# Seven summed block products in place of eight in the second batch's channel up-projection of a fused fp32 kernel

## Chip, cores and metric

The kernel runs on one core of one Trainium2 chip. The metric is the device time of one execution in microseconds (us); lower is better.

## The reference, cut to what matters

Windowed attention over two batches of 768 tokens feeds a gated unit with a spatial mixing matrix, and that feeds a low-rank token mix and a channel network. The change is in the channel network alone:

```python
u = x + (x.T @ U @ V).T                            # (2, 768, 512)
ch = np.maximum(u @ w_ch1, 0.0) @ w_ch2            # w_ch1 512 x 2048, w_ch2 2048 x 512
return u + ch
```

All of it is fp32. The kernel splits each operand into a rounded high part and a low remainder and forms a product from three matrix products: high by high, high by low, low by high.

## The kernel before

The 2048 hidden channels are 16 chunks of 128 (NCH, line 29). The list `seq` (line 821) runs over batch 0's chunks and then batch 1's, 32 steps n in all. In a step, `m4(n, j, bank)` (line 857) makes the hidden activations of one chunk for one half j of the tokens: 4 blocks of 128 input channels by 3 products, 12 matmuls of 384 columns with the weights stationary and `X[b]` moving. ScalarE then writes the rounded ReLU, and VectorE the low part (lines 864 and 865). `m5(n, t)` (line 867) multiplies 128 tokens of the hidden chunk by the chunk's rows of w_ch2: 3 matmuls of 512 columns that accumulate over the 16 chunks in PSUM bank 2+t. After a batch's last chunk VectorE adds y and SyncE stores the result (lines 874 and 875). Banks 0 and 1 take the two halves of m4. The loop of lines 973 to 988 emits m4 of step n and then the six m5 of step n-1.

The weights come from HBM as 64-bit numbers. `ch_decode` (line 839) turns a chunk into fp32, kept in `P["f"]` for both batches; this work ends in batch 0. `ch_split` (line 846) splits a chunk again for each of its two uses: two pieces of 512 columns, in each a rounding on ScalarE and a subtraction on GpSimd, into one of three slots of `P["wch"]`. The first 512 columns of a slot are w_ch1 (`c1`), the other 512 w_ch2 (`c2`).

Order within an engine is the order of emission; engines wait for one another through semaphores alone. The class `Plan` (lines 66 to 189) decides at which point background work such as these splits is put into the engines' streams. It books every instruction on an account of its engine with a price (lines 107 to 120: for VectorE 1.04 ns an element and 70 ns, for GpSimd 2.2 ns an element and 100 ns), with no term for two engines that hinder each other. After each group of three matmuls `tick` (line 162) emits chains, in the order in which they were added, whose engine is booked no more than 400 ns past TensorE's account. `flush` (line 180) emits whatever is left of some chains, one instruction of each in turn.

Of the kernel before, what the change touches and what calls it, by code (L numbers as in the profile page):

```python
# [20 lines left out]
KB = 4  # L21
# [171 lines left out]
def kernel(ctx: ExitStack, tc: tile.TileContext, qk, qt, kn, vab, vn_, gl_,  # L193
# [11 lines left out]
    def body(dense, sb, pp):  # L205
# [5 lines left out]
        def tl(tag, n, name):  # L211
            t = sb.tile([128, n], F32, tag=tag, name=f"{name}_{int(dense)}")
            plan.home[t.tensor.name] = tag
            return t
# [23 lines left out]
        def mm3(o_, l_, r, first, last):  # L238
            mm(o_, l_[0], r[0], first, False)
            mm(o_, l_[0], r[1], False, False)  # L240
            mm(o_, l_[1], r[0], False, last)
            tick()
# [580 lines left out]
        def f_place(c):  # L823

            if c == 0:
                t_ = tl(T_SP, N_SP, "f0")
                P["f"] = [t_[:, 1024 * n:1024 * n + 1024] for n in range(9)]
            elif c == 9:
                t_ = tl("stg", 3072, "f1")
                P["f"] += [t_[:, 1024 * n:1024 * n + 1024] for n in range(3)]  # L830
            elif c == 12:
                P["f"] += [tl(T_WK, N_WK, "f2")[:, 0:1024]]
            elif c == 13:
                t_ = tl(T_UT, N_UT, "f3")
                P["f"] += [t_[:, 1024 * n:1024 * n + 1024] for n in range(3)]
# [3 lines left out]
        def ch_decode(c):  # L839
            f_place(c)  # L840
            f, rw = P["f"][c], P["raw"][c % 2]
            ld = plan.add([o_dma(rw.bitcast(I32), w_ch[c].bitcast(I32))], decoded.get(c - 2, []))
            decoded[c] = [plan.add(decode(rw[:, 1024 * j:1024 * j + 1024], f[:, 512 * j:512 * j + 512]), [ld])
                          for j in range(2)]

        def ch_split(n):
            c = seq[n][1]
            w = [t[:, n % 3] for t in P["wch"]]
            split[n] = [plan.add(splits(w[0][:, 512 * j:512 * j + 512], w[1][:, 512 * j:512 * j + 512],
                                        P["f"][c][:, 512 * j:512 * j + 512], A, G), [decoded[c][j]])  # L850
                        for j in range(2)]

        def chv(n):
            w = [t[:, n % 3] for t in P["wch"]]
# [12 lines left out]
        def m5(n, t):  # L867
            b, c = seq[n]
            _, c2 = chv(n)
            y = P["y"]  # L870
            mm3(bank[2 + t], [P["h1"][n % 2][l][:, 128 * t:128 * t + 128] for l in range(2)], c2,
                n % NCH == 0, n % NCH == NCH - 1)
            if n % NCH == NCH - 1:
                V.tensor_tensor(out=y[b][:, t], in0=bank[2 + t], in1=y[b][:, t], op=ALU.add)
                SP.dma_start(out[b, 128 * t:128 * t + 128, :], y[b][:, t])


        lns, gs = {}, []
# [56 lines left out]
        for t in range(NB):  # L935
# [12 lines left out]
                t3(0, 2 * t - 4, bank[4])  # L948
                t3(0, 2 * t - 3, bank[5])
            tick()  # L950
        P["h1"] = [tl(f"win1{n}", 2048, f"h1{n}") for n in range(2)]
        P["h1"] = [[t[:, l * S:(l + 1) * S] for l in range(2)] for t in P["h1"]]
        flush(split[0])
        m4(0, 0, bank[0])
        t1(1, NB - 1, bank[7])
# [14 lines left out]
        for t in range(3, 6):  # L970
            t3(1, t, bank[5 + t - 3])
        ch_decode(3)
        for n in range(1, 2 * NCH):
            if 1 < n and n + 2 < NCH:
                ch_decode(n + 2)
            if n >= 2:
                flush(split[n])
                m4(n, 0, bank[0])
                tick()
                m4(n, 1, bank[1])  # L980
                tick()
            if n + 1 < 2 * NCH:
                ch_split(n + 1)
            for t in range(NB):
                m5(n - 1, t)
                tick()
        for t in range(NB):
            m5(2 * NCH - 1, t)
        assert not plan.chains

    program(False)
# [56 lines left out]
```

## Time and profile before

| what | us |
|---|---|
| median of 3 runs | 535.81 |
| lowest and highest of them | 533.86 and 538.69 |
| the profiled execution, its own time | 532.87 |
| span of the profiled execution | 531.1 |

The time of an execution holds 1.8 us around the span. PE is TensorE, PEld its weight loads, DVE VectorE, ACT ScalarE, POOL GpSimd, SP SyncE. A row such as "402.31 4.33 PE ... x24" gives the start in us from the span's start, the length of the merged run, and the number of instructions. Nearly all of the kernel's instructions bear line 56, that of a helper, so groups are told apart by the names of their tiles: `bank<-x,wch` is m4, `bank<-wch,h` is m5, `wch` is a weight split, `h` is an eviction of m4.

### The profile page before, as it was taken

How to read it: one execution, taken by the hardware profiler on the slowest of the kernel's cores; microseconds unless marked ns; L12 is line 12 of the kernel's file. 1: busy time of each engine (PE TensorE's matmuls, PEld its weight loads, DVE VectorE, ACT ScalarE, POOL GpSimd, SP SyncE). 2: the span in 40 equal slices, each digit the busy share in tenths (PEclk: the TensorE clock that was granted, in tenths of full speed). 3: DMA queues.
4: the chain of work that ended last, by engine and by line, in shares of the span. 5: the costliest groups of instructions: out<-in, count | busy, mean ns of one | idle time of the engine just before them, and what ended most of it. 6: DMA issues, size and time to landing. Idle time of an engine off the chain costs nothing.

```text
span 531.1 us, 7975 instructions
## 1 busy us (share of the span) xinstructions
PE 504.7 (95%) x2916; PEld 447.5 (84%) x2916; DVE 304.6 (57%) x734; ACT 213.0 (40%) x513; POOL 180.8 (34%) x207
## 2 busy tenths in 40 slices
PE   5768999799999999999999999999999999999994
PEld 4557877689899999888988989899898998989893
DVE  8797789845599743697798867764141101111013
ACT  4878878522454203654444243342212212122120
POOL 5587656610246103220043242423323233231310
PEclk9998999999999999999999999999999999999998
DMA  8657562300421202230126242420030000000003
GB/s 301 220 153 266 167 217 82 121 1 1 122 77 56 61 0 67 112 141 11 69 79 210 107 160 91 148 79 1 0 120 1 0 1 1 1 0 1 0 3 124
DMA packets 13520, 44.74 MB, mean 84 GB/s; under 512 B 1568, under 2 KB 3744, under 8 KB 11424
## 3 DMA queue, kind: packets, MB, share of 16 engines
q1 hardware_dynamic: 13328, 44.14, 24.3%
q8 instruction: 25, 0.41, 0.3%
q14 instruction: 23, 0.19, 0.1%
q10 hardware_dynamic: 144, 0.00, 0.0%
HBM read 40.99 MB, written 3.15 MB: 83 GB/s over the span
## 4 chain that ended last, share of the span: by engine, by line
PE 88%; DVE 8%; ACT 1%; issue 1%; DMA 1%; POOL 0%; ACTq 0%
PE bank L56 88%; DVE prob L56 2%; DVE sm L56 1%; DVE rawin L56 1%; DVE y L56 1%; DVE ptb L56 1%; DMA ni<-in_gl_dram 1%; DVE masks L56 1%; DVE bias L56 1%; ACT prob L56 1%; DVE x L56 0%; ACT ptb L56 0%; ACT vn L56 0%; POOL vn L56 0%; DVE stg L56 0%
## 5 line engine op out<-in xcount | busy, mean ns | idle before, releaser
L56 POOL TENSOR_TENSOR wch<-f,wch 128x512 fp32r<-128x512 f32 x64 | 86.6, 1374 | 212.9 <-ACT wch L56 212.9
L56 PE MATMUL bank<-wch,h 128*128 128x512 f32 x576 | 139.5, 396 | 0.0
L56 PE MATMUL bank<-x,wch 128*128 128x384 f32 x768 | 139.1, 336 | 0.0
L56 PEld LDWEIGHTS bank<-x,wch 128*128 128x128 f32 x768 | 134.5, 188 | 3.1
L56 PEld LDWEIGHTS bank<-wch,h 128*128 128x128 f32 x576 | 107.8, 188 | 23.3
L56 DVE SCALAR_TENSOR_TENSOR h<-bank,h 128x384 fp32r<-128x384 f32 x64 | 35.6, 556 | 141.4 <-ACT h L56 141.4
L56 ACT ACTIVATE h<-bank 128x384 fp32r<-128x384 f32 x64 | 31.5, 492 | 179.3 <-PE bank L56 179.3
L56 POOL TENSOR_SCALAR prob<-prob,sm 128x232 f32<-128x232 f32 (+1 forms) x96 | 47.2, 509 | 32.0 <-ACT prob L56 24.4
L56 PE MATMUL bank<-wsp,vn 128*128 128x384 f32 x288 | 53.2, 339 | 0.9 <-DVE vn L56 0.4
L56 ACT ACTIVATE prob<-prob,sm 128x232 f32<-128x232 f32 (+1 forms) x96 | 44.4, 463 | 21.9 <-DVE sm L56 21.8
L56 PEld LDWEIGHTS bank<-wsp,vn 128*128 128x128 f32 x288 | 49.5, 188 | 2.0 <-DVE vn L56 0.7
L56 DVE TENSOR_SCALAR f<-f 128x512 f32<-128x512 f32 (+1 forms) x64 | 41.4, 684 | 9.6 <-ACT f L56 9.3
L56 DVE SCALAR_TENSOR_TENSOR f<-raw,f 128x512 int32<-128x512 int32 x64 | 43.9, 726 | 0.1
L56 PE MATMUL bank<-ident,prob 128*128 128x128 f32 (+1 forms) x176 | 29.0, 288 | 12.4 <-POOL prob L56 4.6
L56 PE MATMUL bank<-win,x 128*128 128x512 f32 x144 | 39.1, 406 | 0.0
L56 PEld LDWEIGHTS bank<-ident,prob 128*128 128x128 f32 (+1 forms) x176 | 20.1, 140 | 21.8 <-POOL prob L56 12.6
L56 ACT ACTIVATE wch<-f 128x512 fp32r<-128x512 f32 x64 | 36.9, 624 | 1.0 <-DVE f L56 1.0
L56 PE MATMUL bank<-wo,x 128*128 128x512 f32 x144 | 35.3, 395 | 0.0
L56 PE MATMUL bank<-x,win 128*128 128x384 f32 x192 | 33.6, 336 | 0.0
L56 PEld LDWEIGHTS bank<-x,win 128*128 128x128 f32 x192 | 33.3, 188 | 0.1
L56 DVE CUSTOM_DVE_ANT_0 prob<-bank,bias 128x232 f32<-128x232 f32 (+1 forms) x96 | 31.5, 369 | 1.5 <-PE bank L56 1.5
L56 PE MATMUL bank<-raw 64*128 64x232 f32 (+1 forms) x192 | 26.7, 423 | 5.6 <-DMA raw<-in_qk_dram 4.9
(87 smaller groups left out, 500.2 us busy)
## 6 DMA issues: line engine op xcount, KB each, us to landing
raw<-in_w_ch_dram SPq DMA_DIRECT2D x16, 1024.0 KB, 4.8
raw<-in_qk_dram SPq DMA_DIRECT2D x20, 360.0 KB, 3.8
vals<-in_vab_dram SPq DMA_DIRECT2D x10, 512.0 KB, 4.3
out_dram<-y SPq DMA_DIRECT2D x12, 256.0 KB, 2.2
stg<-in_w_in_dram SPq DMA_DIRECT2D x5, 512.0 KB, 4.9
stg<-in_w_sp_dram SPq DMA_DIRECT2D x3, 768.0 KB, 5.2
stg<-in_w_out_dram SPq DMA_DIRECT2D x4, 512.0 KB, 3.8
raw<-in_qk_dram SPq DMA_DIRECT2D x4, 256.0 KB, 3.6
```

Source lines behind the costliest of these rows:

```text
L56: return f(*a, **kw)
```

## The change

Steps 18 to 31 (from `SEVEN` on) are taken in seven pairs q = 0 to 6. The weights of two chunks and the tokens of batch 1 are each seen as a 2 by 2 block matrix (two chunks by two halves of the input channels; two halves of the input channels by two halves of the tokens), and the product of the two is formed by Strassen's seven products of sums. Each product has two blocks of 128 input channels, so 6 matmuls of 384 columns. Steps 0 to 17 keep m4.

- `x_sums`, added to the plan in step 14, forms the five sums or differences of token blocks, high and low parts separately, then together: six tensor-tensor instructions of 384 columns for each, five on VectorE and one on GpSimd. The next sum's chain starts when the one before has been emitted. `x_operands`, in step 16, splits them into high and low: for each sum two roundings on ScalarE and one subtraction on VectorE and one on GpSimd. They are flushed at the head of step 17.
- `w_sums(q)` forms and splits seven weight blocks a pair in five chains (5 VectorE instructions of 256 columns, and 2 + 3 splits of 512 and 256 columns). The first pair's are added in step 17, each later pair's at the beginning of the pair before.
- `ch_split` then splits w_ch2 alone.
- `m4_seven` emits products 5, 4, 3, 2, 1, 6, 7, in alternating banks 0 and 1; VectorE, ScalarE and GpSimd put them together through SBUF (`tmp`). The m5 of the pair before are put between the products: 12 for a pair, 6 for the first one, whose seventh place is taken by a `ch_split`.

The diff, without its empty lines:

```diff
--- before.py
+++ after.py
@@ -829,7 +829,9 @@
                 t_ = tl("stg", 3072, "f1")
                 P["f"] += [t_[:, 1024 * n:1024 * n + 1024] for n in range(3)]
             elif c == 12:
-                P["f"] += [tl(T_WK, N_WK, "f2")[:, 0:1024]]
+                t_ = tl(T_WK, N_WK, "f2")
+                P["f"] += [t_[:, 0:1024]]
+                P["wk"] = t_[:, 1024:1536]
             elif c == 13:
                 t_ = tl(T_UT, N_UT, "f3")
                 P["f"] += [t_[:, 1024 * n:1024 * n + 1024] for n in range(3)]
@@ -843,12 +845,12 @@
             decoded[c] = [plan.add(decode(rw[:, 1024 * j:1024 * j + 1024], f[:, 512 * j:512 * j + 512]), [ld])
                           for j in range(2)]
-        def ch_split(n):
+        def ch_split(n, js=(0, 1)):
             c = seq[n][1]
             w = [t[:, n % 3] for t in P["wch"]]
             split[n] = [plan.add(splits(w[0][:, 512 * j:512 * j + 512], w[1][:, 512 * j:512 * j + 512],
                                         P["f"][c][:, 512 * j:512 * j + 512], A, G), [decoded[c][j]])
-                        for j in range(2)]
+                        for j in js]
         def chv(n):
             w = [t[:, n % 3] for t in P["wch"]]
@@ -868,11 +870,156 @@
             b, c = seq[n]
             _, c2 = chv(n)
             y = P["y"]
-            mm3(bank[2 + t], [P["h1"][n % 2][l][:, 128 * t:128 * t + 128] for l in range(2)], c2,
-                n % NCH == 0, n % NCH == NCH - 1)
-            if n % NCH == NCH - 1:
+            last = n % NCH == NCH - 1
+            if n < SEVEN:
+                h = [P["h1"][n % 2][l][:, 128 * t:128 * t + 128] for l in range(2)]
+            else:
+                h = [x[:, 128 * (t % 3):128 * (t % 3) + 128] for x in hblock(n, t // 3)]
+            mm3(bank[2 + t], h, c2, n % NCH == 0, last)
+            if last:
                 V.tensor_tensor(out=y[b][:, t], in0=bank[2 + t], in1=y[b][:, t], op=ALU.add)
                 SP.dma_start(out[b, 128 * t:128 * t + 128, :], y[b][:, t])
+        def use(n, t, new):
+            if new:
+                flush(split[n])
+            m5(n, t)
+        SEVEN = NCH + 2
+        SUMS = "5432167"
+        HB, USE = [(0, 1), (1, 0), (1, 1), (0, 0)], [(0, 1), (0, 0), (1, 0), (1, 1)]
+        def o_tt(eng, o_, a, b_, op):
+            return KEY[eng], lambda: eng.tensor_tensor(out=o_, in0=a, in1=b_, op=op)
+        def hblock(n, j):
+            q = (n - SEVEN) // 2
+            x = (4 * q + HB.index((n % 2, j)) + 4) % 5
+            if x < 4:
+                w = P["ht"][x // 2][:, 768 * (x % 2):768 * (x % 2) + 768]
+                return w[:, 0:384], w[:, 384:768]
+            return [P["ht"][l][:, 1536:1920] for l in range(2)]
+        def xblock(b, k, j):
+            return [X[b][l][:, 2 * k:2 * k + 2, 384 * j:384 * j + 384] for l in range(2)]
+        def x_sums():
+            raw = [tl(f"win0{l}", 2048, f"xsum{l}") for l in range(2)]
+            two, tmp_ = [], {}
+            for n, (name, a, b_, op) in enumerate((("4", (1, 0), (0, 0), ALU.subtract), ("3", (0, 1), (1, 1), ALU.subtract),
+                                                   ("1", (0, 0), (1, 1), ALU.add), ("6", (0, 0), (0, 1), ALU.add),
+                                                   ("7", (1, 0), (1, 1), ALU.add))):
+                t = raw[n // 2][:, 768 * (n % 2):768 * (n % 2) + 768] if n < 4 else None
+                if t is None:
+                    t = [raw[l][:, 1536:1536 + 384] for l in range(2)]
+                else:
+                    t = [t[:, 0:384], t[:, 384:768]]
+                tmp_[name] = t
+                u = [bsp[:, 0:384], bsp[:, 384:768]]
+                ops = []
+                for k in range(2):
+                    ah, al = (x[:, k] for x in xblock(1, *a))
+                    bh, bl = (x[:, k] for x in xblock(1, *b_))
+                    ops += [o_tt((G, V)[k], u[k], al, bl, op), o_tt(V, t[k], ah, bh, op), o_tt(V, t[k], t[k], u[k], ALU.add)]
+                two.append(plan.add(ops, two[-1:]))
+            return two, tmp_
+        def x_operands(two, tmp_):
+            P["xb"] = {"2": [xblock(1, 0, 0)[l] for l in range(2)], "5": [xblock(1, 1, 1)[l] for l in range(2)]}
+            places = [t[:, 1536 * n:1536 * n + 1536] for t in (tl("x00", KB * S, "xc0"), tl("x01", KB * S, "xc1"))
+                      for n in range(2)] + [tl("uv", 2 * S, "xc2")]
+            ready = []
+            for p, (c, name) in zip(places, zip(two, ("4", "3", "1", "6", "7"))):
+                hi, lo = (p[:, 768 * l:768 * l + 768].rearrange("p (k t) -> p k t", k=2) for l in range(2))
+                P["xb"][name] = [hi, lo]
+                ready.append(plan.add([op for k in range(2) for op in splits(hi[:, k], lo[:, k], tmp_[name][k], A, (V, G)[k])],
+                                      [c]))
+            return ready
+        def wblocks(q):
+            if q % 2 == 0:
+                return [[P["wa"][l][:, 256 * i:256 * i + 256] for i in range(7)] for l in range(2)]
+            return [[P["wch"][l][:, i // 2, 256 * (i % 2):256 * (i % 2) + 256] for i in range(6)]
+                    + [P["wa"][l][:, 1792:2048]] for l in range(2)]
+        WB = {"2": 0, "5": 1, "1": 2, "7": 3, "6": 4, "3": 5, "4": 6}
+        def w_sums(q, before):
+            n0 = SEVEN + 2 * q
+            f0, f1 = (P["f"][seq[n][1]] for n in (n0, n0 + 1))
+            a11, a12, a21, a22 = f0[:, 0:256], f0[:, 256:512], f1[:, 0:256], f1[:, 256:512]
+            t0, t1_, t2_ = bsp[:, 0:512], P["wk"], bsp[:, 512:768]
+            hi, lo = wblocks(q)
+            def two(i):
+                return [(wa[:, 256 * i:256 * i + 512] if q % 2 == 0 else wc[:, i // 2, 0:512])
+                        for wa, wc in zip(P["wa"], P["wch"])]
+            return [plan.add(ops, before[i:i + 1]) for i, ops in enumerate((
+                [o_tt(V, t0[:, 0:256], a21, a22, ALU.add), o_tt(V, t0[:, 256:512], a11, a12, ALU.add)]
+                + splits(*two(0), t0, A, G),
+                splits(hi[6], lo[6], a22, A, G),
+                splits(hi[5], lo[5], a11, A, G),
+                [o_tt(V, t1_[:, 0:256], a11, a22, ALU.add), o_tt(V, t1_[:, 256:512], a12, a22, ALU.subtract)]
+                + splits(*two(2), t1_, A, G),
+                [o_tt(V, t2_, a21, a11, ALU.subtract)] + splits(hi[4], lo[4], t2_, A, G)))]
+        def m4_seven(q, wait, behind):
+            n0 = SEVEN + 2 * q
+            t_ = P["tmp"]
+            s5, s4, s3, c12, c21, z, c22, c11 = (t_[:, 384 * i:384 * i + 384] for i in range(8))
+            blocks = wblocks(q)
+            share = [len(behind) * i // 7 for i in range(8)]
+            def h_out(i, src):
+                hi, lo = hblock(n0 + HB[i][0], HB[i][1])
+                A.activation(out=r_(hi), in_=src, func=AF.Relu)
+                V.scalar_tensor_tensor(out=r_(lo), in0=src, scalar=0.0, in1=hi, op0=ALU.max, op1=ALU.subtract)
+            for i, m in enumerate(SUMS):
+                if i in wait:
+                    flush(wait[i])
+                bk = bank[i % 2][:, 0:384]
+                for k in range(2):
+                    mm3(bk, [blocks[l][WB[m]][:, 128 * k:128 * k + 128] for l in range(2)],
+                        [P["xb"][m][l][:, k] for l in range(2)], k == 0, k == 1)
+                if m == "5":
+                    A.activation(out=s5, in_=bk, func=AF.Copy)
+                elif m == "4":
+                    A.activation(out=s4, in_=bk, func=AF.Copy)
+                elif m == "3":
+                    V.tensor_tensor(out=c12, in0=bk, in1=s5, op=ALU.add)
+                    A.activation(out=s3, in_=bk, func=AF.Copy)
+                    G.tensor_tensor(out=s5, in0=s4, in1=s5, op=ALU.subtract)
+                    h_out(0, c12)
+                elif m == "2":
+                    V.tensor_tensor(out=c21, in0=bk, in1=s4, op=ALU.add)
+                    V.tensor_tensor(out=z, in0=s3, in1=bk, op=ALU.subtract)
+                    h_out(1, c21)
+                elif m == "1":
+                    V.tensor_tensor(out=c22, in0=bk, in1=z, op=ALU.add)
+                    V.tensor_tensor(out=c11, in0=bk, in1=s5, op=ALU.add)
+                elif m == "6":
+                    V.tensor_tensor(out=c22, in0=bk, in1=c22, op=ALU.add)
+                else:
+                    V.tensor_tensor(out=c11, in0=bk, in1=c11, op=ALU.add)
+                    h_out(2, c22)
+                for f in behind[share[i]:share[i + 1]]:
+                    f()
+                    tick()
+            h_out(3, c11)
         lns, gs = {}, []
@@ -948,8 +1095,8 @@
                 t3(0, 2 * t - 4, bank[4])
                 t3(0, 2 * t - 3, bank[5])
             tick()
-        P["h1"] = [tl(f"win1{n}", 2048, f"h1{n}") for n in range(2)]
-        P["h1"] = [[t[:, l * S:(l + 1) * S] for l in range(2)] for t in P["h1"]]
+        P["h1t"] = [tl(f"win1{n}", 2048, f"h1{n}") for n in range(2)]
+        P["h1"] = [[t[:, l * S:(l + 1) * S] for l in range(2)] for t in P["h1t"]]
         flush(split[0])
         m4(0, 0, bank[0])
         t1(1, NB - 1, bank[7])
@@ -970,22 +1117,44 @@
         for t in range(3, 6):
             t3(1, t, bank[5 + t - 3])
         ch_decode(3)
-        for n in range(1, 2 * NCH):
+        for n in range(1, SEVEN):
             if 1 < n and n + 2 < NCH:
                 ch_decode(n + 2)
+            if n == NCH:
+                ready = x_operands(two, tmp_)
+            if n == SEVEN - 1:
+                flush(ready)
+                P["wa"] = [tl(f"win0{l}", 2048, f"wa{l}") for l in range(2)]
+                ws = w_sums(0, [])
             if n >= 2:
                 flush(split[n])
                 m4(n, 0, bank[0])
                 tick()
                 m4(n, 1, bank[1])
                 tick()
-            if n + 1 < 2 * NCH:
+            if n == NCH - 2:
+                flush(decoded[NCH - 1] + decoded[NCH - 2])
+                two, tmp_ = x_sums()
+            if n + 1 < SEVEN:
                 ch_split(n + 1)
             for t in range(NB):
                 m5(n - 1, t)
                 tick()
-        for t in range(NB):
-            m5(2 * NCH - 1, t)
+        P["ht"], P["tmp"] = P["h1t"], tl(T_VN[0][0], N_VN, "tmp")
+        steps = [(lambda t=t: m5(SEVEN - 1, t)) for t in range(NB)]
+        for n in range(SEVEN, 2 * NCH, 2):
+            q, wait = (n - SEVEN) // 2, {i: ws[k:k + 1] for k, i in enumerate((0, 1, 2, 4, 5))}
+            ch_split(n, (1,))
+            steps.insert(6, lambda n=n: ch_split(n + 1, (1,)))
+            if n + 2 < 2 * NCH:
+                ws = w_sums(q + 1, ws)
+            m4_seven(q, wait, steps)
+            steps = [(lambda n=n + e, t=3 * j + i, new=(j, i) == (USE[2 * e][1], 0): use(n, t, new))
+                     for e, j in USE for i in range(3)]
+        for f in steps:
+            f()
+            tick()
         assert not plan.chains
     program(False)
```

## Rows read from the trace of the kernel before

**Rows 1.** The page: busy time of each engine, and the chain that ended last.
```profile
PE 504.7 (95%) x2916; PEld 447.5 (84%) x2916; DVE 304.6 (57%) x734; ACT 213.0 (40%) x513; POOL 180.8 (34%) x207
...
PE 88%; DVE 8%; ACT 1%; issue 1%; DMA 1%; POOL 0%; ACTq 0%
```

**Rows 2.** Chain of waits from 300 us: start, length, what.
```profile
299.78 220.44 PE bank L56 x1104
...
520.25 0.69 DVE y L56
```

**Rows 3.** Timeline, 373 to 402 us: start, length, engine, out<-in, count, idle before.
```profile
373.72 0.56 DVE L56 SCALAR_TENSOR_TENSOR h<-bank,h 128x384 fp32r<-128x384 f32 x1 [1.52 <-ACT h L56]
374.29 2.58 POOL L56 TENSOR_TENSOR wch<-f,wch 128x512 fp32r<-128x512 f32 x2 [5.81 <-ACT wch L56]
...
385.59 4.33 PE L56 MATMUL bank<-x,wch 128*128 128x384 f32 x24
387.87 0.49 ACT L56 ACTIVATE h<-bank 128x384 fp32r<-128x384 f32 x1 [4.75 <-PE bank L56]
388.39 0.56 DVE L56 SCALAR_TENSOR_TENSOR h<-bank,h 128x384 fp32r<-128x384 f32 x1 [5.72 <-ACT h L56]
...
389.75 4.36 PE L56 MATMUL bank<-wch,h 128*128 128x512 f32 x18
...
390.34 1.14 ACT L56 ACTIVATE wch<-f 128x512 fp32r<-128x512 f32 x2
...
390.95 3.89 DVE L56 TENSOR_TENSOR y<-bank,y 128x512 f32<-128x512 f32 x6
391.04 2.58 POOL L56 TENSOR_TENSOR wch<-f,wch 128x512 fp32r<-128x512 f32 x2 [5.78 <-ACT wch L56]
...
393.94 4.33 PE L56 MATMUL bank<-x,wch 128*128 128x384 f32 x24
...
398.11 4.36 PE L56 MATMUL bank<-wch,h 128*128 128x512 f32 x18
...
402.31 0.86 PE L56 MATMUL bank<-x,wch 128*128 128x384 f32 x4
```

**Rows 4.** Stretch of one step: length, then busy us (count) of PE, PEld, DVE, ACT, POOL; clock.
```profile
373.00:381.40 8.40, 8.40 (x44) 7.58 (x44) 1.12 (x2) 2.02 (x4) 2.58 (x2) 1.00 0.00 0
```

**Rows 5.** Timeline, 171 to 174 us: DVE and POOL together.
```profile
170.83 0.56 DVE L56 TENSOR_TENSOR x<-u,x 128x384 fp32r<-128x384 f32 x1
...
171.29 2.61 POOL L56 TENSOR_TENSOR x<-u,x 128x384 fp32r<-128x384 f32 x2 [0.79 <-ACT x L56]
171.31 0.42 DVE L56 TENSOR_SCALAR stg<-stg 128x512 int32<-128x512 int32 x1
171.66 1.37 DVE L56 TENSOR_TENSOR x<-u,x 128x384 fp32r<-128x384 f32 x1
...
172.95 1.50 DVE L56 SCALAR_TENSOR_TENSOR stg<-stg 128x512 int32<-128x512 int32 x1
```

**Rows 6.** Tile x: DVE, then POOL; durations min/median/max in ns.
```profile
L56 DVE TENSOR_TENSOR x<-u,x x8: 544/550/1368, 166.2 to 209.8; 128x384 fp32r<-128x384 f32 x8
...
L56 POOL TENSOR_TENSOR x<-u,x x8: 1021/1184/1342, 161.4 to 210.1; 128x384 fp32r<-128x384 f32 x8
```

**Rows 7.** A group of one shape: busy us, mean ns of one, idle before.
```profile
L56 DVE TENSOR_TENSOR uvk<-stg 128x192 fp32r<-128x192 f32 x1 | 0.4, 359 | 0.4 <-ACT stg L56 0.4
```

**Rows 8.** Stretches of the attention stage, columns as in rows 4.
```profile
28.00:32.00 4.00, 1.83 (x22) 1.26 (x18) 3.96 (x18) 3.49 (x12) 4.00 (x6) 1.00 0.81 265
...
40.00:42.00 2.00, 0.84 (x5) 0.66 (x6) 2.00 (x6) 1.57 (x6) 1.20 (x2) 0.90 1.00 300
42.00:45.00 3.00, 3.00 (x16) 2.43 (x16) 1.98 (x7) 2.23 (x7) 2.25 (x5) 0.50 0.67 271
```

**Rows 9.** Timeline of PE, 36 to 48 us.
```profile
40.77 0.61 PE L56 MATMUL bank<-ident,prob 128*104 128x128 f32 x4 [2.31 <-POOL prob L56]
41.78 1.06 PE L56 MATMUL bank<-ident,prob 128*104 128x128 f32 x4 [0.39 <-DVE ptb L56]
```

## The prediction

> **What bounds the kernel now.** The first view is the page's busy times: TensorE is busy for 95% of the span, VectorE for 57%, ScalarE for 40%, GpSimd for 34% [rows 1]. The second is the chain that ended last: 88% of it is TensorE, and from 300 us to the end it is one run of 220.44 us of matmuls without a gap, and then six additions of y [rows 2]. The third is the timeline of batch 1's first steps. A half of m4 never waits: the 24 matmuls that begin at 385.59 are followed at 389.75 by the 18 of m5, and these at 393.94 by the next 24 [rows 3]. So a matmul of 384 columns takes (389.75 - 385.59)/24 = 173.3 ns, in the next step (398.11 - 393.94)/24 = 173.8 ns; I use 173.6. One of 512 columns takes (393.94 - 389.75)/18 = 232.8 ns. A step lasts 8.37 us. The fourth is the stretch of one step: from 373 us on, GpSimd works 2.58 us of 8.4 and VectorE 1.1, at a granted clock of 1.00 [rows 4]. TensorE is the bound, and what the other engines are given costs nothing as long as it is done when TensorE asks for it.
>
> **What goes.** A pair had 2 x 24 matmuls of m4 and gets 7 x 6: six fewer. Seven pairs save 42 x 173.6 ns = 7.29 us. The m5 stay as they are, and so does the tail: the last six m5 still run one after the other, each with its addition and its store behind it [rows 2].
>
> A page of the Trainium skill (TensorE: Matmul & The Clock Gate, section "Back-to-back issue gap") gives N/2.4 + 2.5 ns, which would be 162.5 ns for 384 columns and a saving of 6.83 us. The trace has 173.6 ns, and that is used.
>
> **What is added in steady pairs (2 to 6).** A pair takes 42 x 173.6 + 36 x 232.8 ns = 15.7 us of TensorE. GpSimd gets four subtractions of 512 columns at 1.29 [rows 3], three of 256 (about 0.75 each, on the line through 1.29 for 512 and 1.02 for 384 [rows 3, 6]) and one of 384: 8.4 us. ScalarE gets four roundings of 512 at 0.57, three of 256 at less, and seven evictions at 0.49 [rows 3]: under 7.5 us. VectorE gets eleven evictions at 0.56 and five sums of 256 at about 0.42: 8.3 us. All fit. A bank has to be free for the product after next; between the two lie another product (1.04 us) and two to four m5 (0.70 each). An eviction begins 0.20 us after the moment at which the next matmul could start (387.87 against 385.59 + 12 x 0.1736 = 387.67) and takes 0.56 [rows 3]; with two in a row and 0.15 for the way back it is 1.5 us against 2.4 or more. Only from product 7 to the next pair's product 5 is it the same bank, 0: 0.20 + 0.56 + 0.15 = 0.9 us against two m5, 1.40. I charge nothing. Were that cover gone, each of the five seams would cost up to 0.9.
>
> **The seam between pairs 0 and 1.** Here the seven places hold six m5 and a split, so no matmul lies between product 7 and product 5 in bank 0: 0.9 us, once. Lower bound 0.6 (the eviction alone), upper 2.2 (VectorE first waits for one GpSimd instruction of 1.29).
>
> **What is added ahead of pair 0** is the largest term. Between 374.28, when VectorE has done the eviction of step 14 and GpSimd begins its splits [rows 3], and the third matmul of pair 0's first product at 402.31 + 0.35 = 402.66, there are 28.4 us. In them go the 30 tensor-tensor instructions of `x_sums`, the 10 subtractions of `x_operands`, three chunks' splits, and the first chain of `w_sums(0)`. VectorE's busy time alone would allow it. But nearly all of these read two operands from SBUF, and the trace shows what that means. At 171.66 a VectorE subtraction of two SBUF operands begins 0.37 us into a GpSimd one; it lasts 1.37 us where its like lasts 0.56 or 0.55, and the two GpSimd subtractions around it last 2.61 instead of 2 x 1.02; the next two-operand instruction of VectorE, at 172.95, takes 1.50 [rows 5, 6]. Instructions with one operand in PSUM are not held: the six additions of y from 390.95 keep the pace of the matmuls, and the two splits at 391.04 beside them take 2.58 us as ever [rows 3]. So two-operand work of VectorE and GpSimd's work run one after the other.
>
> This is also what the Trainium skill says (SBUF — State Buffer, section "Who interferes with whom"): a VectorE instruction with two SBUF inputs contends with a GpSimd instruction that reads SBUF. It speaks against this change, and by it the work would be serial throughout; the trace agrees with 1.37 us.
>
> The serial sum: VectorE 25 + 5 instructions of 384 at 0.48 (a following one starts 0.48 after, 171.31 - 170.83 [rows 5]) = 14.4; GpSimd four of the five in `x_sums` (the first can run earlier, GpSimd was idle 5.81 us [rows 3]) and five in `x_operands` at 1.02 = 9.2; six splits at 1.29 = 7.7; the first chain of weight sums, two VectorE sums of 256 (0.42, between 0.36 for 192 [rows 7] and 0.55 for 384) and a subtraction, 2.1. Together 33.4 us for 28.4: 5.0 us late. Nothing in it can be put off: `x_sums` and `x_operands` are flushed ahead of step 17, and in-order queues keep the rest behind them. The planner books 0.47 and 0.95 us with no contention, so it emits as if all were in time.
>
> Where TensorE sees it: VectorE's eviction of step 16 (normally at 388.39) and its six additions are queued behind the last sums, ScalarE's eviction behind the rounding of the fifth sum (which needs VectorE), and behind those the splits for step 17. I expect a wait of some 1.7 us at m4 of step 17, at 394. The rest, 3.3 us, comes at pair 0's first product, whose weights wait in turn behind VectorE's five subtractions of `x_operands`. Bounds: 0, if the engines overlap as well as their busy times allow (both then have spare time); and 8.1, with each of the 30 at its full 0.55 (2.1 more) and the first GpSimd sum inside the window (1.0). I take 5.0, since rows 5 show the serial order at the very pair of instructions that is added.
>
> **Sum.** -7.29 + 0.9 + 5.0 = -1.4 us. The profiled execution, 532.87, becomes 531.5. The median of the runs lies 2.94 above it; by the median the forecast is 535.81 - 1.4 = 534.4.
>
> **Rivals.**
> A. The preparation hides: VectorE and GpSimd fall late, but against deadlines with slack (an h of step 16 is not used before 398). For it: 20 of the sums are already on their way in steps 14 and 15, and the busy times fit. Against: rows 5. Then -7.29 + 0.9 = -6.4: 529.4.
> B. Slower than before: TensorE stands still ahead of pair 0 and drops to half clock. The trace shows it once: after 2.31 us of idleness at 38.4 and 0.39 at 41.4 [rows 9] the clock is 0.90 in 40 to 42 and 0.50 in 42 to 45 [rows 8], 0.2/0.5 + 3.0 = 3.4 us at half rate, 1.7 us of work lost. With the upper bound of 8.1 us that is -7.29 + 0.9 + 8.1 + 1.7 = +3.4: 539.2. Its point: all waiting together must pass 7.29 us, that is 6.4 ahead of pair 0, or 4.7 if the clock drops. Against: at 28 to 32 TensorE worked 1.83 of 4 us and kept 1.00 [rows 8], and my waits are in two places.
> C. The seams of the steady pairs wait too, since an eviction on VectorE stands behind an `h` subtraction of two SBUF operands (the sums c12 to c22 lie in SBUF, where m4's eviction read PSUM) and that behind a GpSimd split. Half a us at five seams, and as forecast otherwise: -1.4 + 2.5 = +1.1: 536.9. For it: eight GpSimd instructions a pair. Against: at product 7 the sum c11 is emitted ahead of that subtraction.
>
> A page of the Trainium skill (TensorE: Matmul & The Clock Gate, "The HAM clock gate") also says that idleness of TensorE lowers its clock; rows 8 and 9 agree, with the clock of 0.50, and by it B's 1.7 us would be due.
>
> **How the numbers follow.** Forecast 0.50, A 0.23, B 0.12, C 0.15. The likeliest is 534.4; its own range, with a wait ahead of pair 0 of 3 to 6.5 us, is 532.4 to 535.9. The range for 8 in 10 takes A in, with half of what runs differ among themselves (533.86 to 538.69) below it, and C and the lower part of B: 528.0 to 538.0. A measurement of this kernel can tell about 1%, 5.4 us, from no change. Faster by more than that are A and no more than a little of the forecast: 0.25. Slower by more is the far part of B and what noise adds: 0.10. Within 1%: 0.65.
>
> **What would show it.** Right: 42 fewer matmuls of 384 columns, at 173 to 174 ns each; VectorE instructions on the sums of 1 us and more where GpSimd runs beside them; a gap of TensorE at 394 and a larger one before the first summed product; one of about 0.9 us between pairs 0 and 1, none at the later seams; TensorE's end 1 to 2 us earlier. Wrong: a step 17 and a pair 0 without gaps (A); a clock of 0.50 near 405 (B); gaps at each seam (C); or matmuls of another pace, which would move the first term itself.

## The result, and the profile after

The changed kernel takes 540.25 us (median of 20 runs, 537.11 to 541.81), the one before 534.65 in the runs beside it (median of 20, 532.14 to 538.81). The ratio is 1.0094, 95% interval 1.0074 to 1.0115: slower by 0.9% (5.6 us between the medians), where 1.4 us less was forecast, and outside the range of 528.0 to 538.0. The profiled execution took 540.65 us, with a span of 538.8.

The page, engines and shares of the chain, against [rows 1]:

```profile
PE 504.5 (94%) x2874; PEld 444.7 (83%) x2874; DVE 382.7 (71%) x848; ACT 233.7 (43%) x565; POOL 220.2 (41%) x245
...
PE 81%; DVE 10%; ACT 3%; DMA 2%; issue 2%; POOL 1%; SPq 0%; ACTq 0%; DVEq 0%
```

TensorE has its 42 matmuls fewer (2916 to 2874), and is busy as long as before: 504.5 against 504.7 us. Its share of the chain falls from 88% to 81%. VectorE has 78 us more to do.

Where did the saving go? The chain of waits from 300 us on (start, length, what), against [rows 2], cut to the pieces that matter:

```profile
299.96 75.49 PE bank L56 x378
...
377.12 1.48 DVE xsum L56
...
398.96 0.53 ACT xc L56
...
402.03 14.87 PE bank L56 x64
...
417.67 0.88 DVE bsp L56
...
419.42 8.17 PE bank L56 x33
427.61 0.57 DVE tmp L56
...
428.22 99.73 PE bank L56 x489
```

Before, the run of matmuls was whole from 300 to 520 us. Now the chain leaves TensorE at 375.47 and runs mostly through VectorE's token sums (`xsum`, `bsp`) until 399. It leaves TensorE again at 417 and 427.6. From 428.22 it is matmuls to the additions at the end: the steady pairs wait for nothing.

The stretches around the breaks (length, busy us and count of PE, PEld, DVE, ACT, POOL, then the granted clock):

```profile
391.00:396.20 5.20, 5.20 (x25) 4.22 (x23) 5.20 (x7) 0.91 (x2) 3.44 (x3) 1.00 0.00 0
396.20:400.40 4.20, 0.18 (x1) 0.00 (x0) 4.17 (x9) 1.96 (x5) 2.08 (x2) 0.86 0.00 0
400.40:406.00 5.60, 4.97 (x14) 4.47 (x15) 5.57 (x12) 1.02 (x2) 2.83 (x3) 0.50 0.73 281
...
417.90:419.40 1.50, 0.00 (x0) 0.00 (x0) 1.10 (x2) 1.26 (x4) 0.35 (x1) 1.00 0.00 0
419.40:423.90 4.50, 4.48 (x16) 4.20 (x17) 2.83 (x4) 1.28 (x3) 3.96 (x4) 0.62 0.00 0
```

TensorE stands still from 396.2 to 400.4 while VectorE works throughout. Before the stop is over its granted clock falls to 0.50, that is 1.2 GHz, half of full (so the stop's mean is 0.86). It stays there until 406, with 14 matmuls in 5.6 us. The same happens on a smaller scale behind the stop at 418, where the mean is 0.62 until 423.9.

An account of TensorE's time, from the same matmul in both kernels (step 13's first, 360.43 before, 362.70 after; the 2.27 us between lie in the attention stage, where nothing changed) to the last addition of y (523.74 before, 531.48 after). The difference is 7.74 - 2.27 = 5.47 us:

| where | us |
|---|---|
| 42 matmuls of 384 columns fewer, at 173.6 ns | -7.29 |
| stop ahead of step 17, 396.22 (392.03 + 18 x 0.2328) to 400.44 | +4.22 |
| step 17's 24 matmuls take 7.35 us in place of 4.17: 0.94 of waiting for a low part, the rest half clock | +3.18 |
| stop in pair 0, ahead of product 2 | +1.99 |
| half clock behind it | +1.68 |
| seam between pairs 0 and 1: a stop of 0.84, and a first product of 1.15 us in place of 1.04 | +0.93 |
| what is left: some 0.5 a pace of 175 ns in place of 173.6, 0.2 at pair 0's first product (its six matmuls take 1.25 us in place of 1.04) | +0.76 |

(The view of TensorE's waits gives 4.1, 0.6, 1.8 and 0.7 us for the four waits, since it counts from the modelled end of a matmul; the account counts from start to start.)

The first term came nearly as worked out: a steady pair lasts 15.76 us where 15.7 was forecast and two steps took 16.73. Product 5 of pairs 5 and 6 begins at these times:

```profile
491.36 1.21 PE L56 MATMUL bank<-x,wch 128*128 128x384 f32 x6
...
507.12 1.21 PE L56 MATMUL bank<-x,wa 128*128 128x384 f32 x6
```

**The stop ahead of step 17.** The timeline at the beginning of the sums (start, length, engine, out<-in):

```profile
376.56 3.21 POOL L56 TENSOR_TENSOR wch<-f,wch 128x512 fp32r<-128x512 f32 x2 [4.85 <-ACT wch L56]
377.12 1.48 DVE L56 TENSOR_TENSOR xsum<-xsum,bsp 128x384 f32<-128x384 f32 x1
378.52 1.66 DVE L56 TENSOR_TENSOR bsp<-x 128x384 f32<-128x384 f32 x1
379.72 1.33 POOL L56 TENSOR_TENSOR bsp<-x 128x384 f32<-128x384 f32 x1
380.11 1.37 DVE L56 TENSOR_TENSOR xsum<-x 128x384 f32<-128x384 f32 x1
```

Beside GpSimd's work a sum of 0.55 us takes 1.4 to 1.7, and GpSimd's two splits take 3.21 instead of 2.58 [rows 3]. The group of the sums of tile `xsum` says it in one line (min/median/max):

```profile
L56 DVE TENSOR_TENSOR xsum<-x x10: 544/1357/1656, 376.5 to 404.9; 128x384 f32<-128x384 f32 x10
```

And the end of the chain, where the wait reaches TensorE:

```profile
398.39 0.54 DVE L56 TENSOR_TENSOR xsum<-xsum,bsp 128x384 f32<-128x384 f32 x1
...
398.96 0.52 ACT L56 ACTIVATE xc<-xsum 128x384 fp32r<-128x384 f32 x1 [2.15 <-DVE xsum L56]
...
399.39 0.47 ACT L56 ACTIVATE h<-bank 128x384 fp32r<-128x384 f32 x1
...
399.76 1.14 ACT L56 ACTIVATE wch<-f 128x512 fp32r<-128x512 f32 x2
...
400.44 1.01 PE L56 MATMUL bank<-x,wch 128*128 128x384 f32 x2 [4.06 <-ACT wch L56]
```

ScalarE stands 2.15 us before the rounding `xc<-xsum` at 398.96, the eighth of ten, because the sum that it rounds, the fourth, is late. Behind that rounding stand the eviction of step 16 (`h<-bank`) and the weights of step 17 (`wch<-f`, in the kernel before at 390.34, which is 392.61 on this kernel's time), and for these TensorE waits.

**The stop in pair 0** is a second one of the same kind, on the same engine:

```profile
417.34 0.91 POOL L56 TENSOR_TENSOR wa<-f,wa 128x256 fp32r<-128x256 f32 x1
417.59 0.95 DVE L56 TENSOR_TENSOR bsp<-f 128x256 f32<-128x256 f32 x1
...
418.57 0.42 ACT L56 ACTIVATE wch<-bsp 128x256 fp32r<-128x256 f32 x1 [0.24 <-DVE bsp L56]
418.89 0.85 ACT L56 ACTIVATE tmp<-bank 128x384 f32<-128x384 f32 x2
419.42 0.47 PE L56 MATMUL bank<-x,wa 128*128 128x384 f32 x1 [1.82 <-ACT tmp L56]
```

ScalarE's copies of products 4 and 3 out of their banks (`tmp<-bank`) stand behind roundings of pair 1's weights, which wait for VectorE's weight sums, and these for GpSimd (0.95 in place of 0.41). Product 2 needs bank 1, so TensorE waits for the copy of product 4.

### The profile page after: what moved, and what is told of

Same layout as the page of the kernel before. It is cut to its first block, busy times and chain, and to the rows that moved or that the text cites. A ratio compares the mean times of both kernels' runs of the same rounds, so it can differ in the third digit from the quotient of the medians.

```text
span 538.8 us, 8155 instructions
## 1 busy us (share of the span) xinstructions
PE 504.5 (94%) x2874; PEld 444.7 (83%) x2874; DVE 382.7 (71%) x848; ACT 233.7 (43%) x565; POOL 220.2 (41%) x245
## 4 chain that ended last, share of the span: by engine, by line
PE 81%; DVE 10%; ACT 3%; DMA 2%; issue 2%; POOL 1%; SPq 0%; ACTq 0%; DVEq 0%
PE bank L56 81%; DVE xsum L56 3%; DVE prob L56 2%; DMA stg<-in_w_sp_dram 1%; ACT prob L56 1%; DVE sm L56 1%; DVE rawin L56 1%; DVE y L56 1%; DVE bsp L56 1%; DMA ni<-in_gl_dram 1%; DVE bias L56 1%; ACT vn L56 0%; DVE masks L56 0%; ACT ptb L56 0%; DVE ptb L56 0%
## 5 line engine op out<-in xcount | busy, mean ns | idle before, releaser
L56 PE MATMUL bank<-wch,h 128*128 128x512 f32 x576 | 145.7, 397 | 0.0
L56 POOL TENSOR_TENSOR wch<-f,wch 128x512 fp32r<-128x512 f32 (+1 forms) x56 | 77.5, 1399 | 155.1 <-ACT wch L56 152.6
L56 PE MATMUL bank<-x,wch 128*128 128x384 f32 x468 | 88.4, 343 | 5.3 <-ACT wch L56 4.1
L56 PEld LDWEIGHTS bank<-x,wch 128*128 128x128 f32 x468 | 84.1, 192 | 8.7 <-ACT wch L56 4.5
L56 ACT ACTIVATE h<-bank 128x384 fp32r<-128x384 f32 x36 | 17.7, 491 | 78.8 <-PE bank L56 78.8
L56 DVE TENSOR_TENSOR tmp<-bank,tmp 128x384 f32<-128x384 f32 x42 | 22.6, 552 | 29.9 <-PE bank L56 29.9
L56 PE MATMUL bank<-win,x 128*128 128x512 f32 x144 | 40.4, 416 | 0.0
L56 DVE SCALAR_TENSOR_TENSOR h<-bank,h 128x384 fp32r<-128x384 f32 x36 | 19.8, 551 | 23.6 <-ACT h L56 23.6
L56 ACT ACTIVATE h<-tmp 128x384 fp32r<-128x384 f32 x28 | 14.7, 524 | 49.6 <-DVE tmp L56 34.8
L56 ACT ACTIVATE wch<-f 128x512 fp32r<-128x512 f32 (+1 forms) x56 | 32.5, 610 | 3.3 <-DVE f L56 3.3
```

Source lines behind the costliest of these rows:

```text
L56: return f(*a, **kw)
```

## Experiments

Medians, with the ratio to the kernel before in the runs beside it; two kernels were executed once each. All that is said of waits and clocks is read from one profiled execution of each kernel.

| kernel | us | ratio (95%) |
|---|---|---|
| e1_early | 533.18 | 0.9975 (0.9955 to 0.9996) |
| e2_nolow, one execution | 532.41 | |
| e3_seam | 537.14 | 1.0054 (1.0029 to 1.0078) |
| e5_nox, one execution | 528.07 | |
| e7_onv | 534.26 | 1.0010 (0.9978 to 1.0043) |
| e8_early_seam | 533.53 | 0.9988 (0.9965 to 1.0011) |
| e9_early_seam_onv | 534.93 | 1.0017 (0.9988 to 1.0047) |
| e10_late | 528.81 | 0.9903 (0.9870 to 0.9936) |
| e11_hold | 530.10 | 0.9924 (0.9889 to 0.9958) |
| e6_late | 538.11 | 1.0063 (1.0034 to 1.0092) |
| e13_late_opnd | 530.72 | 0.9935 (0.9910 to 0.9959) |

### Is it the token sums, and do the two engines hold each other up?

**e5_nox** leaves the sums out.

```diff
-                ready = x_operands(two, tmp_)
+                P["xb"] = {m: xblock(1, 0, 0) for m in "1234567"}
+                ready = []
...
-                two, tmp_ = x_sums()
+                pass
```

> Leaves out the token sums and their splits: every product reads the same unsummed token block. What stays are the weight sums, the seven products, their evictions and the m5. Theory: no gap before step 17 and a full clock there; the gap of 2.0 us in pair 0 (evictions on ScalarE behind roundings of the next pair's weights) can stay with its half clock; the time falls by 7.4 us or more, to 533 or below. Rival (the weight sums or the extra instructions are what costs): over 537.

Measured: 528.07 us. All that the view of TensorE's waits has left between 262 us and the end is the seam:

```profile
PE bank L56 <- DVE tmp L56: 0.7, 1, 0.7
```

The stop in pair 0 is gone as well, though the weight sums have the same place in the program: pair 0's begin 7.5 us ahead of its first product (396.24 and 403.79), in the changed kernel 3.0 us (409.0 and 411.99). So it, too, came from work that the token sums had made late. The token sums cost some 12 us (540.25 to 528.07, a single execution), though none of their instructions runs on TensorE. As e5_nox takes work from VectorE, GpSimd and ScalarE at once, it does not tell which of them it was.

**e2_nolow** leaves out GpSimd's subtractions for three chunks.

```diff
-   P["f"][c][:, 512 * j:512 * j + 512], A, G), [decoded[c][j]])
+   P["f"][c][:, 512 * j:512 * j + 512], A, G)[:1 if n in (15, 16, 17) else 2], [decoded[c][j]])
```

> Leaves out the low parts of the weights of steps 15, 16 and 17 (GpSimd's six subtractions of 512 columns beside the token sums), nothing else. Theory (shared port): the VectorE instructions that took 1.3 to 1.7 us beside these six fall to 0.55, VectorE comes some 6 us further by step 17, the gap there falls from 4.2 us to under 1 and the clock stays at full. Rival (VectorE has too much work of its own, no matter what GpSimd does): the durations stay and the gap stays above 3 us.

Measured: 532.41 us. The same line of the view of tile `xsum`:

```profile
L56 DVE TENSOR_TENSOR xsum<-x x10: 545/550/1379, 375.8 to 393.5; 128x384 f32<-128x384 f32 x10
```

The stretch through step 17, with the columns as above:

```profile
381.40:402.00 20.60, 20.60 (x104) 18.54 (x104) 19.48 (x34) 9.63 (x22) 10.29 (x9) 1.00 0.20 77
```

With six GpSimd instructions out of the way, the same VectorE sums have a median of 0.550 us in place of 1.357, the last of this form starts at 393.5 in place of 404.9, and TensorE goes through to 402 without a gap and at full clock. (Stops of 1.0 and 1.7 us in pair 0 stay in the view of its waits.) No instruction of VectorE was taken away, so the rival (too much work of its own) falls.

**e7_onv** tests the same from the other side: it gives VectorE more.

```diff
-   ops += [o_tt((G, V)[k], u[k], al, bl, op), ...
+   ops += [o_tt(V, u[k], al, bl, op), ...
...
-   for op in splits(hi[:, k], lo[:, k], tmp_[name][k], A, (V, G)[k])
+   for op in splits(hi[:, k], lo[:, k], tmp_[name][k], A, V)
```

> The token sums and their low parts entirely on VectorE: GpSimd's five sums and five subtractions go there too, nothing else changes. Theory (two-operand work of the two engines runs one after the other, so only its sum counts): 40 x 0.48 = 19.2 us in place of 30 x 0.48 + 10 x 1.0 = 24.4, so VectorE, although it gets more to do, is done 5 us earlier; the gap of 4.2 us before step 17 falls below 1 and the clock stays, 540.3 becomes 533 to 534. Rival (VectorE simply has too much work, a division between two engines helps it): the gap grows, the time is 541 or more.

Measured: 534.26 us, 6.0 less than the changed kernel, though VectorE has ten instructions more. Step 17 is free of gaps. What was not expected is a new stop, of 3.4 us, at the first summed product:

```profile
403.90:407.30 3.40, 0.16 (x1) 0.00 (x0) 3.25 (x8) 2.24 (x6) 0.00 (x0) 1.00 0.00 0
408.70:412.10 3.40, 3.40 (x10) 3.11 (x11) 3.00 (x4) 1.96 (x5) 3.02 (x4) 0.50 0.00 0
```

The lateness has become smaller and has moved to where the prediction had put most of it: pair 0's first weights. Counted from step 16's first matmul (387.18 here, 387.86 in the changed kernel), the fourth sum is done 4.2 us sooner (394.06 and 398.93), and the last subtraction 2.0 us sooner (405.01 and 407.68).

### How much time, and where in the queue?

**e1_early** adds the token sums one step earlier.

```diff
-            if n == NCH - 2:
+            if n == NCH - 3:
                 flush(decoded[NCH - 1] + decoded[NCH - 2])
```

> The token sums are added to the plan one step earlier (step 13 instead of 14), nothing else. Theory (VectorE and GpSimd share a port for two-operand work, so the token sums end some 7 us late; ScalarE's queue then holds the rounding of the last sums ahead of step 17's weights, TensorE stands for 4.2 us and falls to half clock): with 8.4 us more, the gap of 4.2 us before step 17 and the half clock behind it go, 7.4 us together, and the time falls from 540.3 to about 533. Rival (ScalarE's order alone, whatever the time the sums are given): the gap stays over 3 us and the time within 1.5 us of 540.3.

Measured: 533.18 us, as the theory had it, but not by the way it gave. A stop of 2.5 us ahead of step 17 stays; the clock does not fall:

```profile
390.07 6.52 POOL L56 TENSOR_TENSOR xc<-xsum,xc 128x384 fp32r<-128x384 f32 x5 [2.40 <-ACT xc L56]
390.47 6.54 DVE L56 TENSOR_TENSOR xc<-xsum,xc 128x384 fp32r<-128x384 f32 x5
...
396.93 1.01 DVE L56 SCALAR_TENSOR_TENSOR h<-bank,h 128x384 fp32r<-128x384 f32 x2
...
397.62 1.56 PE L56 MATMUL bank<-x,wch 128*128 128x384 f32 x6 [2.38 <-ACT wa L56]
```

Five subtractions on each engine take 6.5 us side by side. By themselves they would take 2.75 and 5.1 us (5 x 0.55 and 5 x 1.02): so the two do not run one beside the other, and not quite one after the other either. Step 16's low parts, which free bank 0, stand behind VectorE's five and come at 396.93; the matmul starts 0.7 us later. (The view names ScalarE; that instruction wrote pair 0's weights, and the first of VectorE's two, which ends some 0.55 us after 396.93, is what bank 0 waits for.)

**e3_seam** moves a split in the first pair.

```diff
-            steps.insert(6, lambda n=n: ch_split(n + 1, (1,)))
+            steps.insert(6 if q else 0, lambda n=n: ch_split(n + 1, (1,)))
```

> In the first pair the split is put in the first of the seven places instead of the last, so one m5 lies between product 7 and the next pair's product 5. Theory: the gap of 0.82 us between pairs 0 and 1 shrinks to about 0.2 and nothing else changes, 540.3 becomes 539.6. Rival (the gap is not bank 0's release but VectorE's lateness): the gap stays at 0.8.

Measured: 537.14 us, 3.1 less, where 0.7 was expected. The seam is gone, as forecast. But the stop in pair 0 shrinks too, from 1.8 to 0.4 in the view of TensorE's waits, and the half clock behind it does not come: the place of one split in the plan has changed when things come in that pair. Which of ScalarE's instructions made the difference was not followed up.

**e8_early_seam** has both edits.

> The earlier token sums of e1_early and the seam of e3_seam together. Theory: the gap of 2.5 us before step 17 stays, the seam falls from 0.8 to 0.2 and the 1.5 us in pair 0 to some 0.6, as it did in e3_seam: 533.2 - 0.6 - 0.9 = 531.7. Rival (the gains overlap): no better than 532.9.

Measured: 533.53 us: no gain over e1_early. The two stops that stay are 2.5 and 1.0 us, nearly as expected, but this time the first is followed by half clock, which takes 1.2 us back (step 17's 24 matmuls take 5.75 us, in e1_early 4.52). The same stop had left the clock at full in e1_early. The stretch behind it there:

```profile
397.50:402.00 4.50, 4.37 (x24) 4.09 (x25) 4.50 (x9) 0.82 (x3) 3.33 (x4) 1.00 0.60 232
```

And in e8_early_seam:

```profile
398.00:401.40 3.40, 3.27 (x10) 3.20 (x11) 3.40 (x7) 0.33 (x2) 3.29 (x4) 0.50 0.45 175
```

Each is one profiled execution; how often either comes in the timed runs was not seen.

**e9_early_seam_onv** adds e7_onv's edit.

> e8_early_seam, and the token sums entirely on VectorE. Theory: with both, the gap before step 17 falls from 2.5 us to under 0.5; what is left beside the 7.3 us saved is about 1 us: 528 to 529, faster than before by over 1%. Rival: VectorE's load delays the evictions of steps 14 to 17, and the time stays at 531 or above.

Measured: 534.93 us. This theory fell: the gap ahead of step 17 is down to a wait of 0.2, but the stop in pair 0 grows to 4.1 us, with half clock behind it.

```profile
408.18 2.36 DVE L56 TENSOR_TENSOR bsp<-f 128x256 f32<-128x256 f32 x2
...
411.44 0.63 ACT L56 ACTIVATE wch<-f 128x512 fp32r<-128x512 f32 x1 [0.24 <-DVE f L56]
411.98 0.47 ACT L56 ACTIVATE tmp<-bank 128x384 f32<-128x384 f32 x1
...
412.50 1.62 PE L56 MATMUL bank<-xc,wa 128*128 128x384 f32 x6 [3.91 <-ACT tmp L56]
```

Pair 0's weight sums begin only 2.9 us ahead of its first product (402.71 and 405.64), no more than in the changed kernel. And the copy of product 5 at 411.98, which frees bank 0 for the third product, now stands in ScalarE's queue behind roundings of pair 1's weights that wait for VectorE. In the changed kernel that copy came ahead of them (413.43), and only the copy of product 4 stood behind.

**e11_hold** takes those out of the way.

```diff
-            if n + 2 < 2 * NCH:
+            if q == 0:
+                nxt = []
+                steps[3] = lambda f=steps[3], ws=ws: (f(), nxt.extend(w_sums(1, ws)))
+            elif n + 2 < 2 * NCH:
                 ws = w_sums(q + 1, ws)
             m4_seven(q, wait, steps)
+            if q == 0:
+                ws = nxt
```

> e9_early_seam_onv, and the weight sums for pair 1 are added to the plan after the fourth product of pair 0 instead of ahead of the pair. Theory (the gap of 4.1 us in pair 0 of e9_early_seam_onv is ScalarE's copy of product 4 out of bank 1, queued behind roundings that wait for VectorE's weight sums, each held up by a GpSimd split): the gap goes and with it the half clock of 1.7 us; 534.9 becomes 529 to 529.5. Rival (the first pair is too short for its work, wherever it stands): the wait only moves to pair 1's first product, the gaps stay at 3 us or more in all, and the time above 532.

Measured: 530.10 us. The stop of 4.1 us and its half clock are gone. (The copy that it waited for was product 5's out of bank 0, not product 4's; the edit takes the roundings from ahead of both.) A wait of 1.4 is left at pair 1's first product, the place that the rival named, but half of what it asked for. A weight sum of 0.41 us takes 1.50 beside a GpSimd split, and the eviction that frees bank 0 stands behind it.

```profile
413.83 1.53 POOL L56 TENSOR_TENSOR wch<-bsp,wch 128x512 fp32r<-128x512 f32 x1 [1.41 <-ACT wch L56]
...
414.14 1.50 DVE L56 TENSOR_TENSOR bsp<-f 128x256 f32<-128x256 f32 x1
...
415.56 0.54 DVE L56 TENSOR_TENSOR tmp<-bank,tmp 128x384 f32<-128x384 f32 x1
...
416.25 0.94 PE L56 MATMUL bank<-x,wch 128*128 128x384 f32 x4 [1.40 <-DVE tmp L56]
```

**e6_late** starts the summed products two steps later, with the changed kernel otherwise as it is.

```diff
-        SEVEN = NCH + 2
+        SEVEN = NCH + 4
```

> The changed kernel with SEVEN at step 20 alone: six pairs, the sums stay divided between VectorE and GpSimd, added in step 14, the seam as it was. Theory: two steps (16.7 us) more cover the 5 to 7 us of lateness; what is left are the seam of 0.8 us and at most 1 us at step 17; 36 matmuls save 6.25: before less 4.5 to 5.5, 529 to 530. Rival (the division between the engines and the order must change too, as in e10_late): gaps of 3 us or more remain, over 532.

Measured: 538.11 us; the rival was right. Two more steps now lie between step 17 and the first use of a sum, and TensorE stops at step 17 as before, for the same engines:

```profile
PE bank L56 <- ACT wch L56: 4.0, 1, 4.0
PE bank L56 <- DVE tmp L56: 0.7, 1, 0.7
PE bank L56 <- POOL wch L56: 0.6, 1, 0.6
```

A later deadline does not help what is queued in front of something else. The operands are still added in step 16, so their roundings still stand ahead of step 17's weights.

**e13_late_opnd** moves that one line.

```diff
-            if n == NCH:
+            if n == SEVEN - 2:
                 ready = x_operands(two, tmp_)
```

> e6_late with one line more: the token operands are added in step 18 instead of step 16; the sums still begin in step 14 and stay divided between the two engines. Theory as it stands after e6_late (late sums do harm only through the queue: ScalarE's roundings of the last sums stand ahead of the eviction of step 16 and the weights of step 17): the gap of 4.2 us before step 17, the 1.2 behind it and the half clock go, the seam of 0.8 stays, 538.1 becomes 531 to 532 or, if nothing else comes late, 530. Rival (the sums themselves, on VectorE ahead of the evictions of step 16, hold bank 0): a gap of 2 us or more stays at step 17.

Measured: 530.72 us, 7.4 less than e6_late, and less than the kernel before (ratio 0.9935). The stop of 4.2 us, its second wait and the half clock are gone. Of the rival's a wait of 0.9 for VectorE's eviction is left, one step later, beside the seam:

```profile
PE bank L56 <- DVE h L56: 0.9, 1, 0.9
PE bank L56 <- DVE tmp L56: 0.7, 1, 0.7
```

Two things have changed on the way. Step 17's weights are rounded at 391.39, ahead of the fourth sum, which is done at 394.79: they no longer wait for it. And with the subtractions of `x_operands` gone from between the sums, the fourth sum is itself done 2.9 us sooner than in e6_late, counted from step 16's first matmul (8.1 and 11.0 us after it). How much of the stop each of the two takes away was not separated.

**e10_late** has all of it: the sums early, entirely on VectorE, the seam, and six pairs.

> e9_early_seam_onv with the summed products from step 20 on, six pairs in place of seven: 36 matmuls fewer instead of 42 (6.25 us instead of 7.29), with two steps more for the preparation. Theory: no gap over 0.3 us is left; time before less 6.0, about 528.6. If e9_early_seam_onv has gaps of over 1.3 us in all, this one is faster, otherwise it is slower by up to 1.0.

Measured: 528.81 us, ratio 0.9903 (0.9870 to 0.9936), the lowest median of all: 1.0% below the kernel before, where the changed kernel was 0.9% above it. From 380 to 500 us TensorE waits once:

```profile
PE bank L56 <- DVE h L56: 0.2, 1, 0.2
```

## Why the prediction was wrong, point by point

The first term held: 42 matmuls fewer, and steady pairs of 15.76 us without a stop, so rival C (waits at every seam) fell. The seam between pairs 0 and 1 was forecast at 0.9 and measured 0.93, with bank 0 as its cause (e3_seam takes it away). The mechanism of the largest term held in the main: two-operand work of VectorE and GpSimd slows both down, nearly as if it ran one after the other (in e1_early 6.5 us for what would be 7.5 in turn, 5 x 0.48 + 5 x 1.02). e2_nolow and e7_onv show it from both sides. A rule of the Trainium skill (SBUF — State Buffer, "Who interferes with whom") spoke against the change: a VectorE instruction with two SBUF inputs contends with a GpSimd one that reads SBUF. It is borne out by 1.357 against 0.550 us.

What failed is the step "Where TensorE sees it" and the sum that hung on it. It put 1.7 us at step 17 and 3.3 at pair 0's first product. Measured were 4.2 + 0.9 at step 17, no stop at pair 0's first product, and 2.0 at product 2: 7.2 us of waiting where 5.0 were taken, within the bounds of 0 and 8.1. The order of the queue had been read rightly on ScalarE (its eviction and step 17's weights behind the rounding of a late sum, though it was the fourth and not the fifth). On VectorE it had not: the six additions of y, at 400.37, run ahead of the fifth sum, which ends at 406. The price at step 17 was too low. The text took the lateness to build up until pair 0 and let step 17 see a third of it. e6_late shows why that is wrong: what TensorE feels is not how late the sums are for their own use, but how late they are when something with an earlier deadline stands behind them. e6_late moves the use by two steps and keeps the stop; e13_late_opnd takes the roundings, and the subtractions that follow them, out of the way, and it goes. The second stop, in pair 0, was not in the prediction at all: it counted whether ScalarE had the time for the weight roundings of the next pair, and not that the copies out of the banks stand behind them.

The other part is the clock. The stops cost 3.9 us more by half clock: 3.18 - 0.94 = 2.2 in step 17 and 1.7 in pair 0. That was rival B, with 1.7 us once, held against it that "my waits are in two places". They were, and each was followed by half clock. The forecast's sum had the clock at nothing, and this is its largest miss: between its -1.4 and the account's +5.5 lie 6.9 us, of which 3.9 are the clock, 2.2 more waiting than taken, and 0.8 what is left in the account. Rival B came nearest, and its sign, a clock of 0.50 near 405, was seen from 400.4 to 406. It moved the time by +3.4, with 8.1 us of waiting and 1.7 of clock, where the account has 7.2 and 3.9. Rival A, that the preparation hides, is what e10_late shows to be possible once order and place are changed.

With the terms as measured, the forecast's own sum reads -7.29 + 0.93 + 7.15 + 3.92 = +4.7; the account's 5.47 holds 0.76 more, the line of what is left.

## What to carry to other kernels

Work that is given to engines with spare time is late not by their busy shares but by what they share and by what stands behind it: find every instruction that will be queued behind the new one, and price the wait at the earliest of their deadlines. Where two engines slow each other down, do not count on dividing work between them: time it on the faster one alone. Add it to the queues only when its inputs will be there. In a kernel like this one a stop of TensorE should be charged with the half clock that can follow it: in these profiles it followed seven of the eight stops of 2.0 us and more, and cost 1.2 to 2.2 us each time.

## What the hardware showed that was not expected

Dividing work between VectorE and GpSimd gained little or nothing: five subtractions on each take 6.5 us side by side (e1_early), where VectorE alone does each of the ten in 0.55 us, 5.5 in all. The row of e7_onv:

```profile
L56 DVE TENSOR_TENSOR xc<-xsum,xc x10: 545/548/559, 390.7 to 404.4; 128x384 fp32r<-128x384 f32 x10
```

What that was worth depended on the rest. Against the changed kernel e7_onv had the fourth sum 4.2 us sooner. But e9_early_seam_onv, which differs from e8_early_seam by this alone, had the last subtraction no sooner (done 10.2 and 10.3 us after step 16's first matmul): three of them took 3.25 us beside GpSimd's splits.

The clock after a stop is not settled by its length alone. Stops of 4.2 us (the changed kernel, e3_seam, e6_late), 4.1 (e9_early_seam_onv) and 3.4 (e7_onv) were followed by half clock each time. One of 2.5 was followed by it in e8_early_seam and not in e1_early, one of 2.0 was in the changed kernel, and those of 1.8 (e2_nolow), 1.5 (e1_early) and 1.6 (e11_hold) were not; all are counted from start to start. What decides between them was not tried.
